# Hash attention and a sigmoid-GELU feed-forward on one Trainium2 core: the first pair of steps with one Strassen level, weight conversion handed out operation by operation, and another order of PSUM banks

## The chip, the cores and the metric

The kernel runs on one core of a Trainium2 chip. The metric is the device time of one execution in microseconds. A core has TensorE (PE, matmuls into PSUM), VectorE (DVE), ScalarE (ACT) and GpSimd (POOL), each with its own queue that it works off in order, and DMA queues that are fed by issuing engines; here nearly all transfers are issued by SyncE (SP), one after the other. Engines wait for each other through semaphores. [...]

## The reference

```python
# q, k, v: (4, 8, 768, 64); proj: (64, 6); w_in: (512, 2048); w_out: (2048, 512), the weights in double precision
q_bucket, k_bucket = ...                      # 6 sign bits of q @ proj and k @ proj, as a number
scores = where(q_bucket == k_bucket, q @ k.T / sqrt(64), -1e9)
attn = softmax(scores) @ v
x = attn.transpose(0, 2, 1, 3).reshape(3072, 512)
h = x @ w_in
return (h * 1 / (1 + exp(-1.702 * h))) @ w_out
```

All arithmetic is float32. The first half of the program is the attention, the second the two products of the feed-forward; the change is in the first of these two.

## The kernel before

**Attention** (to about 316 us). Sixteen pairs of heads; at the end `xT` holds x transposed, 512 x 3072. VectorE normalizes the result of the last pair of heads (`invert`, `norm`, L492 to L506) after PE has started on the feed-forward. The weights come as doubles and are converted to floats by `convert` in chunks of 128 x 512: one load of 512 KB (`raw`, L162), then six VectorE operations (L178 or L180, L182, L186 or L188, L193, L195, L198) and one square on ScalarE (L190). There is one `raw` buffer, so a chunk can be loaded only when L193 and the square of the chunk before it are done. Fourteen chunks of w_in are converted during attention; the last two (`LATE`) and the sixteen of w_out during the feed-forward.

**First product, h = x @ w_in** (`feed_forward`, 316 to 625 us). It is made in three blocks of 1024 tokens, and in each block in eight steps of 128 rows in each half of h, 24 steps in all, numbered n. One level of Strassen-Winograd turns a step into seven products (`product`, L739, each two matmul instructions of 128x128x512), whose operands are sums of quarters of w_in (`in_sums`, on GpSimd) and of x (`sums_b`, on VectorE). Results are gathered in SBUF tiles u, v, c21 and c22 by copies on ScalarE and adds on VectorE (`add`, L749); ScalarE applies the activation (`emit`, L746); GpSimd makes the four outer sums that the second product will want of them (`g_outer`, L219 to L222); and each result goes to HBM (`keep`, L743) on SyncE's queue.

There are two forms of a step. `hidden` (L930) makes all seven products whole. `pair_of_steps` (L828) makes two steps at once, and in it products 2 and 3 of both steps together are done by a second level of Strassen (`nested`, L789): seven small products of 128x128x256 (L800) each in place of four whole products for the two. They want sums of their own, of weights (`nest_w`, on GpSimd) and of x (`nest_x`, on VectorE). They accumulate in only two PSUM banks (pool `inner`, tags a and x), so most small products wait until VectorE has added the one before on the same bank. The first small product of product 3 is made at the end of its pair; the other six are put on the list `behind` and made between the products of the next pair. The completion of v (`done3`) then releases ScalarE's activation and GpSimd's eight outer sums for both steps.

Steps 0 to 19 are ten such pairs, and steps 20 to 23 use `hidden`. Its products take PSUM banks in turn (`bank`, L719): four of the pool `outer` and four of `sets`.

**What orders the work.** The instructions of PE, VectorE, ScalarE and GpSimd run in the order in which the program issues them. Extra work is put between the products at numbered hooks (`on`, L1148): hook 1 stands after a pair's first product, hook 2 after the second, 3 and 4 after the two products 6, 5 after the first small product of product 2, 6 and 7 after the products 7, 8 after the products 5 and their adds, 9 and 10 after the products 4, hook 10 at the very end. The table `todo` says which step gets a conversion, a sum for the second product, and so on. `conversions` (L1093) walks the chunks; it starts the load of the next chunk with the first operations of the present one, and stops twice in a chunk, so that one call issues operations one to three and the next call four to six. SyncE's queue is not written by hand: a planner puts each transfer into it.

Of the kernel before, what the change touches and what calls it, by code (L numbers as in the profile page):

```python
# [8 lines left out]
F32 = mybir.dt.float32  # L9
# [10 lines left out]
P = 128  # L20
# [18 lines left out]
def kernel(  # L39
# [166 lines left out]
    LATE = 2  # L206
# [29 lines left out]
    def in_sums(t):  # L236
        return sums_a(nc.gpsimd, *quarters_in(slice(2 * t * P, (2 * t + 2) * P)))
# [457 lines left out]
    def feed_forward(tag, late=()):  # L695
# [9 lines left out]
        with ExitStack() as fctx:  # L705
# [5 lines left out]
            inner_ctx = fctx.enter_context(ExitStack())  # L711
            inner = inner_ctx.enter_context(tc.tile_pool(name=f"in{tag}", bufs=1, space=PSUM, side="right"))
# [217 lines left out]
            def hidden(sb, mt, mid=(), end=()):  # L930
                n = sb * MT + mt
                first = n not in heads
                a, u = heads.pop(n) if n in heads else head(n)
# [30 lines left out]
                if not first and n + 1 < n1 * MT:  # L964
# [140 lines left out]
            for t in range(NESTED):  # L1105
                sb, at = divmod(t, MT // 2)
                hooks = {}
                steps_of = pair_of_steps(t, hooks)
                if t == 0:
                    next(steps_of)  # L1110
                    yield
                    twice = twice_ctx.enter_context(tc.tile_pool(name=f"tw{tag}", bufs=1, side="right"))
                    wop = fctx.enter_context(tc.tile_pool(name=f"wo{tag}", bufs=1))
                    cv_ctx = fctx.enter_context(ExitStack())
                    cv = cv_ctx.enter_context(tc.tile_pool(name=f"cv{tag}", bufs=1))
                    cps = cv_ctx.enter_context(tc.tile_pool(name=f"cps{tag}", bufs=1, space=PSUM))


                    w_out_sb = wop.tile([P, 4, FC, P], F32, name="w_out_sb")
                    wqs += [w_out_sb[:, 2 * i : 2 * i + 2, MT * k : MT * (k + 1), :] for i in range(2) for k in range(2)]  # L1120
                    wqs += [xT[:, i, 0 : 4 * XT].rearrange("p (h c d) -> p h c d", h=2, d=P) for i in range(3)]

                    order = [8 * k + 4 * c + i for c in range(2) for k in range(2) for i in range(4)]
                    chunks = [(w_out_sb[:, :, fc, :].rearrange("p r x -> p x r"), wo[fc]) for fc in order]
                    steps = conversions(cv, cps, late + chunks)
                    free = [i for i in range(LATE + 1, 3 * MT) if i % MT != MT - 1]
                    for i in (list(range(1, LATE + 1)) if late else []) + free[:FC]:
                        todo[i] = [lambda: next(steps)] * 2
                    low, high = (sums_a(nc.vector, *(x[:, :, F4 * c : F4 * (c + 1), :] for x in wqs)) for c in range(2))
                    first = 2 * MT + 1  # L1130
                    for i, f in enumerate(low):
                        todo[first + i] = todo[first + i] + [f]
                    todo[first + 1] = todo[first + 1] + inner_sums(0)[:2]
                    todo[first + 2] = todo[first + 2] + inner_sums(0)[2:]
                    todo[first + 4] = high + inner_sums(1)
                    todo[first + 5] = inner_sums(2)
                    todo[first + 6] = inner_sums(3)


                    places = [[w_out_sb[:, r, 4:8, :].rearrange("p c d -> p (c d)") for r in range(4)],  # L1140
                              [xT[:, k, XT * j : XT * (j + 1)] for k in (1, 0) for j in range(2)],
                              [xT[:, k, XT * j : XT * (j + 1)] for k, j in ((2, 1), (0, 3), (1, 3), (1, 1))]]
                    places = [[x[:, j * TH : (j + 1) * TH] for x in y for j in range(2)] for y in places]
                    more = nest_x(0, places[0])
                    hooks[3] = more[2] + nest_w(0)
                    hooks[4] = more[3]

                def on(i, fs):  # L1148
                    hooks[i] = hooks.get(i, []) + fs

                if at == 0 and sb > 0:
                    on(1, more[2])
                    on(3, more[3][:2])
                    on(4, more[3][2:])
# [4 lines left out]
                x = todo.pop(2 * t + 1, [])  # L1159
                on(7, x[0:1])  # L1160
                on(9, x[1:2])
                on(10, x[2:])
                if t + 1 < MT // 2:
                    on(5, in_sums(t + 1))
                    on(8, nest_w(t + 1))
                if at == MT // 2 - 1:
                    x = sums_b(nc.vector, *quarters_x(sb + 1))
                    more = nest_x(sb + 1, places[sb + 1])
                    on(8, x[0:1])
                    on(9, x[1:2])  # L1170
                    on(10, x[2:4])
                whole(steps_of)
                yield
            nesting[0] = False
            for n in range(2 * NESTED, 3 * MT):
                sb, mt = divmod(n, MT)
                if n == 2 * NESTED + 1:
# [119 lines left out]
```

## Time and profile before

| | |
|---|---|
| median of three runs | 892.74 us (891.35 to 893.68) |
| profiled execution | 891.65 us, span 889.5 us |
| feed-forward, first product | 316.5 to 624.9 us |
| second product | 624.9 us to the end |

The page of the profile gives for each engine its busy time, for each pair of engines who waited for whom, and groups of instructions by the line that issued them. A row such as `L739 PE MATMUL product<-xT,w_in_sb` names line, engine, operation, output and inputs. In lists in order of time the first two numbers are start and duration in microseconds; in brackets stands the idle time before it on that engine and what ended it. One matmul instruction on floats shows as two records, so a product of two instructions shows as x4 and a small product as x2, and the recorded duration overlaps with the next one's start by 0.16 us.

### The profile page before, as it was taken

How to read it: one execution, taken by the hardware profiler on the slowest of the kernel's cores; microseconds unless marked ns; L12 is line 12 of the kernel's file. 1: busy time of each engine (PE TensorE's matmuls, PEld its weight loads, DVE VectorE, ACT ScalarE, POOL GpSimd, SP SyncE). 2: the span in 40 equal slices, each digit the busy share in tenths (PEclk: the TensorE clock that was granted, in tenths of full speed). 3: DMA queues.
4: the chain of work that ended last, by engine and by line, in shares of the span. 5: the costliest groups of instructions: out<-in, count | busy, mean ns of one | idle time of the engine just before them, and what ended most of it. 6: DMA issues, size and time to landing. Idle time of an engine off the chain costs nothing.

```text
span 889.5 us, 13736 instructions
## 1 busy us (share of the span) xinstructions
PE 858.9 (97%) x4965; PEld 522.4 (59%) x4965; DVE 705.7 (79%) x1068; ACT 340.5 (38%) x567; POOL 324.5 (36%) x291
## 2 busy tenths in 40 slices
PE   9999999999999979999999999989999999999996
PEld 4444444444444435555555554534888888888885
DVE  4589999999999886667866697547797978797786
ACT  5866677766677523433333333333100000000000
POOL 4242243332343463876443333778923100000000
PEclk9999999999999998999999999989999999999998
DMA  5536545665542103554455546566655485477534
GB/s 129 95 58 112 89 82 83 111 109 99 84 83 80 34 25 99 208 194 156 167 193 196 195 157 210 189 208 241 219 230 189 159 225 206 168 223 233 197 105 98
DMA packets 169164, 132.12 MB, mean 149 GB/s; under 512 B 123616, under 2 KB 138112, under 8 KB 163712
## 3 DMA queue, kind: packets, MB, share of 16 engines
q1 hardware_dynamic: 166528, 129.70, 51.2%
q10 hardware_dynamic: 2560, 1.46, 0.7%
q8 instruction: 41, 0.67, 0.3%
q14 instruction: 35, 0.29, 0.1%
HBM read 79.69 MB, written 50.33 MB: 146 GB/s over the span
## 4 chain that ended last, share of the span: by engine, by line
PE 74%; DVE 13%; POOL 4%; issue 4%; DMA 3%; ACT 1%; SPq 0%; ACTq 0%; DVEq 0%; POOLq 0%
PE product L1056 26%; PE ps L432 17%; PE av L465 13%; PE product L739 12%; PE small L800 3%; DMA raw<-in_moe_w_out_dram 3%; DVE xT L1060 1%; DVE v L749 1%; PE dn L486 1%; PE hash L408 1%; DVE w_out_sb L195 1%; POOL t L222 1%; POOL t L221 1%; POOL t L219 1%; DVE bits L182 1%
## 5 line engine op out<-in xcount | busy, mean ns | idle before, releaser
L433 ACT ACTIVATE e<-ps 128x768 f32<-128x768 f32 x192 | 151.3, 812 | 25.6 <-PE ps L432 23.1
L432 PE MATMUL ps<-qT,kT 64*128 64x384 f32 x768 | 155.1, 482 | 0.0
L465 PE MATMUL av<-e,v 128*32 128x385 f32 x1536 | 128.0, 487 | 0.0
L440 POOL TENSOR_TENSOR acc<-e 128x768 f32<-128x768 f32 x32 | 51.8, 1618 | 194.3 <-ACT e L433 174.8
L739 PE MATMUL product<-xT,w_in_sb 128*128 128x512 f32 x208 | 99.7, 607 | 0.0
L739 PE MATMUL product<-t_x,s_in 128*128 128x512 f32 x192 | 91.5, 603 | 4.2 <-DVE w_out_sb L198 4.1
L465 PEld LDWEIGHTS av<-e,v 128*32 128x32 f32 x1536 | 48.5, 109 | 76.3 <-issue 74.6
L432 PEld LDWEIGHTS ps<-qT,kT 64*128 64x128 f32 x768 | 68.0, 187 | 38.5 <-issue 38.4
L219 POOL TENSOR_TENSOR t<-v,u 128x512 f32<-128x512 f32 x24 | 33.3, 1386 | 125.3 <-ACT v L746 125.3
L1069 ACT COPY u<-product 128x256 f32<-128x256 f32 x21 | 7.8, 372 | 174.0 <-PE product L1056 140.8
L432 PE MATMUL ps<-qf,kf 64*128 64x384 bf16 x384 | 62.9, 324 | 0.1
L739 PEld LDWEIGHTS product<-xT,w_in_sb 128*128 128x128 f32 x208 | 40.6, 196 | 33.8 <-issue 31.5
L739 PEld LDWEIGHTS product<-t_x,s_in 128*128 128x128 f32 x192 | 36.9, 193 | 34.8 <-issue 26.6
L441 POOL TENSOR_TENSOR acc<-acc,e 128x768 f32<-128x768 f32 x32 | 55.8, 1744 | 2.5
L446 DVE SCALAR_TENSOR_TENSOR acc<-e 128x768 f32<-128x768 f32 x32 | 47.7, 1490 | 5.1 <-ACT e L433 5.1
L749 DVE TENSOR_TENSOR v<-small,v 128x256 f32<-128x256 f32 x70 | 28.9, 418 | 24.3 <-PE small L800 24.3
L739 PE MATMUL product<-t_x,w_in_sb 128*128 128x512 f32 x96 | 45.2, 593 | 0.0
L749 DVE TENSOR_TENSOR u<-small,u 128x256 f32<-128x256 f32 x70 | 28.5, 417 | 16.3 <-PE small L800 8.0
L432 PEld LDWEIGHTS <-kf 64*128 64x128 bf16 x384 | 18.9, 94 | 35.1 <-issue 6.2
L448 DVE TENSOR_TENSOR acc<-acc,e 128x768 f32<-128x768 f32 x32 | 34.3, 1072 | 3.3
L448 DVE TENSOR_TENSOR acc<-acc,acc 128x768 f32<-128x768 f32 x32 | 31.7, 991 | 6.3 <-POOL acc L441 3.2
L1056 PE MATMUL product<-raw_g,xT 128*128 128x256 f32 x152 | 35.1, 379 | 0.0
(241 smaller groups left out, 1648.6 us busy)
## 6 DMA issues: line engine op xcount, KB each, us to landing
raw_g<-g_dram SPq DMA_DIRECT2D x22, 1024.0 KB
s_in<-g_dram SPq DMA_DIRECT2D x20, 1024.0 KB
g_dram<-t SPq DMA_DIRECT2D x72, 256.0 KB
g_dram<-c SPq DMA_DIRECT2D x48, 256.0 KB
raw<-in_moe_w_in_dram SPq DMA_DIRECT2D x16, 512.0 KB
raw<-in_moe_w_out_dram SPq DMA_DIRECT2D x16, 512.0 KB
v<-in_v_dram SPq DMA_DIRECT2D x32, 192.0 KB
g_dram<-u SPq DMA_DIRECT2D x24, 256.0 KB
```

The costliest lines, as they stand in the source:

```text
L219: return [lambda: eng.tensor_tensor(t1, b12, b11, op=Alu.subtract), lambda: eng.tensor_tensor(b12, b22, b12, op=Alu.subtract), lambda: eng ...
L432: nc.tensor.matmul(ps[:, j, 0:HS], a[hs, keys], m[hs, cols], start=not last, stop=last)
L433: nc.scalar.activation(es[c][:, kt, :, 0:HS], ps[:, :, 0:HS], Act.Exp, scale=1.0 / D**0.5)
L440: nc.gpsimd.tensor_tensor(acc, es[c][:, 0, :, 0:HS], es[c][:, 1, :, 0:HS], op=Alu.add)
L441: nc.gpsimd.tensor_tensor(acc, acc, es[c][:, 2, :, 0:HS], op=Alu.add)
L446: nc.vector.scalar_tensor_tensor(acc, e[0], T * TINY, e[1], op0=Alu.add, op1=Alu.add)
L448: nc.vector.tensor_tensor(acc, acc, x, op=Alu.add)
L465: nc.tensor.matmul(av[D * j + d : D * j + d + 32, :], vt[:, t, j, d : d + 32], es[c][:, t, j, :], start=(t == 0), stop=(t == T - 1))
L739: nc.tensor.matmul(ps, wq[LEFT[i]][:, kc, :], xq[RIGHT[i]][:, kc, :], start=(start and kc == 0), stop=(kc == K2 - 1), skip_group_check=not ...
L749: nc.vector.tensor_tensor(dst, x, y, op=Alu.add)
L800: nc.tensor.matmul(ps[at], wq[LEFT[i]], xq[RIGHT[i]], start=start, stop=True, skip_group_check=not start)
L1056: nc.tensor.matmul(ps, wq[LEFT[i]][:, c, :], gq[RIGHT[i]][:, c, :], start=(c == 0), stop=(c == F4 - 1))
```

## The change

Three things change in `feed_forward`.

1. Steps 0 and 1 are made by `hidden`. They borrow a pool of two banks (`f1`), which is closed after step 1; then the pool `inner` is opened in its place. Only pairs 1 to 9 (`NESTED = range(1, MT + 2)`) use the second level. The sums of x for it, and those of the weights for pair 1, are issued within step 1; those of the weights for pair 0 move to pair 3, since the first pair of the next block uses them. In the new order of SyncE's queue the loads of the two late chunks of w_in stand behind the stores of step 0 and of step 1, and in most pairs the first load of a chunk stands behind one more store, that of u.
2. `conversions` stops after each operation. A chunk takes six calls, at hooks 1, 2, 2, 3, 3, 4 in a pair's first half and 6, 7, 7, 9, 9, 10 in its second, where it was two calls at 2 and 3, or 7 and 9. The last sum of x for a new block moves from hook 10 to hook 1 of the next pair, and the eight inner sums of x are spread over hooks 1 to 9, one at each but hook 3.
3. For steps 21 to 23 the two new bank pools change places: the first (`f2`) lies where `inner` was, the second (`f3`) where the conversion's tiles were. Before, the first lay on the conversion's.

```diff
-            NESTED = 2 * MT // 2 + 2
-            sets, todo, turn = [], {}, [-1]
+            NESTED = range(1, MT + 2)
+            sets = [small_ctx.enter_context(tc.tile_pool(name=f"f1{tag}", bufs=1, space=PSUM, side="right"))]
+            todo, turn = {}, [-1]
...
-                    for at, _ in enumerate(x):
-                        if at == 2:
-                            yield
+                    for _ in x:
+                        yield
                     yield
...
-            for t in range(NESTED):
+            hidden(0, 0, in_sums(1))
+            yield
...
-                        todo[i] = [lambda: next(steps)] * 2
+                todo[i] = [lambda: next(steps)] * 6
...
-                    hooks[3] = more[2] + nest_w(0)
-                    hooks[4] = more[3]
+            more = nest_x(0, places[0])
+            hidden(0, 1, nest_w(1) + more[2], more[3] + todo.pop(1, []))
+            yield
+            small_ctx.close()
+            inner_ctx = fctx.enter_context(ExitStack())
+            inner = inner_ctx.enter_context(tc.tile_pool(name=f"in{tag}", bufs=1, space=PSUM, side="right"))
+            nesting[0] = True
+            for t in NESTED:
...
-                x = todo.pop(2 * t, [])
-                on(2, x[0:1])
-                on(3, x[1:2])
-                on(5, x[2:])
...
+                for n, places_of in ((2 * t, (1, 2, 2, 3, 3, 4)), (2 * t + 1, (6, 7, 7, 9, 9, 10))):
+                    x = todo.pop(n, [])
+                    for i in places_of:
+                        on(i, *x[:1])
+                        x = x[1:]
+                    on(5 if n % 2 == 0 else 10, *x)
...
+                elif t + 1 == MT // 2:
+                    on(5, *nest_w(0))
...
-                    sets += [fctx.enter_context(tc.tile_pool(name=f"f{i}{tag}", bufs=1, space=PSUM)) for i in (1, 2)]
+                    sets[:] = [fctx.enter_context(tc.tile_pool(name=f"f{2 + i}{tag}", bufs=1, space=PSUM, side=side))
+                               for i, side in enumerate(("right", "left"))]
```

More of the change, by code (lines that the diff above doesn't have):

```diff
@@ L710, in feed_forward @@
             outer = fctx.enter_context(tc.tile_pool(name=f"f0{tag}", bufs=2, space=PSUM, side="right"))
-            inner_ctx = fctx.enter_context(ExitStack())
-            inner = inner_ctx.enter_context(tc.tile_pool(name=f"in{tag}", bufs=1, space=PSUM, side="right"))
+            small_ctx = fctx.enter_context(ExitStack())
+            inner = None
             twice_ctx = fctx.enter_context(ExitStack())
@@ L963, in hidden @@
                 keep(sb, mt, 0, u)
-                if not first and n + 1 < n1 * MT:
+                if not first and n + 1 < n1 * MT and (n + 1) // 2 not in NESTED:
                     heads[n + 1] = head(n + 1)
@@ L1099, in conversions, with on @@
                         next(y)
-                    for at, _ in enumerate(x):
-                        if at == 2:
-                            yield
+                    for _ in x:
+                        yield
                     yield
-            for t in range(NESTED):
+            def on(i, *fs):
+                hooks[i] = hooks.get(i, []) + list(fs)
+            hidden(0, 0, in_sums(1))
+            yield
+            twice = twice_ctx.enter_context(tc.tile_pool(name=f"tw{tag}", bufs=1, side="right"))
@@ new lines, in feed_forward @@
+            wop = fctx.enter_context(tc.tile_pool(name=f"wo{tag}", bufs=1))
+            cv_ctx = fctx.enter_context(ExitStack())
+            cv = cv_ctx.enter_context(tc.tile_pool(name=f"cv{tag}", bufs=1))
+            cps = cv_ctx.enter_context(tc.tile_pool(name=f"cps{tag}", bufs=1, space=PSUM))
+            w_out_sb = wop.tile([P, 4, FC, P], F32, name="w_out_sb")
+            wqs += [w_out_sb[:, 2 * i : 2 * i + 2, MT * k : MT * (k + 1), :] for i in range(2) for k in range(2)]
+            wqs += [xT[:, i, 0 : 4 * XT].rearrange("p (h c d) -> p h c d", h=2, d=P) for i in range(3)]
@@ new lines, in feed_forward @@
+            order = [8 * k + 4 * c + i for c in range(2) for k in range(2) for i in range(4)]
+            chunks = [(w_out_sb[:, :, fc, :].rearrange("p r x -> p x r"), wo[fc]) for fc in order]
+            steps = conversions(cv, cps, late + chunks)
+            free = [i for i in range(LATE + 1, 3 * MT) if i % MT != MT - 1]
+            for i in (list(range(1, LATE + 1)) if late else []) + free[:FC]:
+                todo[i] = [lambda: next(steps)] * 6
+            low, high = (sums_a(nc.vector, *(x[:, :, F4 * c : F4 * (c + 1), :] for x in wqs)) for c in range(2))
@@ new lines, in feed_forward @@
+            first = 2 * MT + 1
+            for i, f in enumerate(low):
+                todo[first + i] = todo[first + i] + [f]
+            todo[first + 1] = todo[first + 1] + inner_sums(0)[:2]
+            todo[first + 2] = todo[first + 2] + inner_sums(0)[2:]
+            todo[first + 4] = high + inner_sums(1)
+            todo[first + 5] = inner_sums(2)
+            todo[first + 6] = inner_sums(3)
+            places = [[w_out_sb[:, r, 4:8, :].rearrange("p c d -> p (c d)") for r in range(4)],
+                      [xT[:, k, XT * j : XT * (j + 1)] for k in (1, 0) for j in range(2)],
+                      [xT[:, k, XT * j : XT * (j + 1)] for k, j in ((2, 1), (0, 3), (1, 3), (1, 1))]]
@@ L1106, in feed_forward @@
+            places = [[x[:, j * TH : (j + 1) * TH] for x in y for j in range(2)] for y in places]
+            more = nest_x(0, places[0])
[6 more added lines that the diff above has]
+            for t in NESTED:
                 sb, at = divmod(t, MT // 2)
@@ L1107, in feed_forward @@
                 hooks = {}
[L1108 to L1127, printed above, removed]
-                        todo[i] = [lambda: next(steps)] * 2
[L1129 to L1144, printed above, removed]
-                    hooks[3] = more[2] + nest_w(0)
-                    hooks[4] = more[3]
@@ L1148, in on @@
[L1148 to L1154, printed above, removed]
-                x = todo.pop(2 * t, [])
-                on(2, x[0:1])
-                on(3, x[1:2])
-                on(5, x[2:])
[L1159 to L1162, printed above, removed]
+                if at == 0:
+                    on(1, x_sums[3], more[2][0])
+                    for i, f in zip((2, 4, 5, 6, 7, 8, 9), more[2][1:] + more[3]):
+                        on(i, f)
@@ L1166, in feed_forward @@
                 if at == MT // 2 - 1:
-                    x = sums_b(nc.vector, *quarters_x(sb + 1))
+                    x_sums = sums_b(nc.vector, *quarters_x(sb + 1))
                     more = nest_x(sb + 1, places[sb + 1])
[L1169 to L1172, printed above, removed]
+                    for i in range(3):
+                        on(8 + i, x_sums[i])
+                whole(pair_of_steps(t, hooks))
@@ L1173, in feed_forward @@
                 yield
-            nesting[0] = False
-            for n in range(2 * NESTED, 3 * MT):
+            turn[0] = -1
+            for n in range(2 * NESTED.stop, 3 * MT):
                 sb, mt = divmod(n, MT)
-                if n == 2 * NESTED + 1:
+                if n == 2 * NESTED.stop + 1:
                     assert not behind
```

5 lines of the change are left out of this document (3 added, 2 removed).

## The prediction

> **What bounds the kernel now.** I read the page's busy times, then who waited for whom on PE, then the order in time of every engine in the first half of the feed-forward (316 to 625 us), the only stretch that the change touches.
>
> ```profile
> PE 858.9 (97%) x4965; PEld 522.4 (59%) x4965; DVE 705.7 (79%) x1068; ACT 340.5 (38%) x567; POOL 324.5 (36%) x291
> PE small L800 <- DVE v L749: 9.1, 9, 2.0
> PE small L800 <- issue: 5.2, 1, 5.2
> PE product L739 <- DVE w_out_sb L198: 4.1, 1, 4.1
> ```
>
> PE is busy 97% of the span, so time is won only where it waits: 9.1 us in nine waits for VectorE's adds, 5.2 in the first pair of steps, 4.1 in the bank wait of step 21. The two long ones cost more than their idle time (busy time by stretch; the last three columns are granted clock, DMA share and GB/s):
>
> ```profile
> 330.50:333.00 2.50, 0.00 (x0) 0.01 (x1) 2.50 (x6) 0.00 (x0) 2.34 (x5) 0.82 0.01 3
> 335.00:337.00 2.00, 2.00 (x4) 0.87 (x3) 0.42 (x1) 0.00 (x0) 1.92 (x2) 0.50 0.35 131
> 337.00:339.00 2.00, 2.00 (x4) 0.98 (x3) 0.00 (x0) 0.49 (x2) 1.84 (x5) 0.52 0.00 0
> 588.00:590.00 2.00, 0.75 (x1) 0.50 (x2) 1.90 (x3) 0.00 (x0) 1.92 (x3) 0.53 0.68 253
> 594.00:596.00 2.00, 2.00 (x4) 0.74 (x4) 0.00 (x0) 0.21 (x1) 1.70 (x2) 0.77 0.73 270
> ```
>
> The clock is at half from about 332.1 to 338.9 and from 588.1 to 594.9 (0.82 over 2.5 us is 0.9 us at half, 0.77 over 2.0 is 0.9, and so on): 6.8 us each time. PE is at work from 333.0 and 589.25 in them, so half of 5.9 and of 5.7 us, 2.9 and 2.8, is lost besides the idle time.
>
> **Part A: the first two steps (to the start of pair 2).** PE in order of time:
>
> ```profile
> 316.45 3.70 PE L739 MATMUL product<-xT,w_in_sb 128*128 128x512 f32 x8
> 333.02 1.19 PE L800 MATMUL small<-w_out_sb,w 128*128 128x256 f32 x2 [5.16 <-issue]
> 341.18 1.88 PE L739 MATMUL product<-t_x,w_in_sb 128*128 128x512 f32 x4
> 342.90 0.59 PE L800 MATMUL small<-w_out_sb,w_in_sb 128*128 128x256 f32 x2
> 343.33 1.88 PE L739 MATMUL product<-t_x,w_in_sb 128*128 128x512 f32 x4
> 369.12 1.88 PE L739 MATMUL product<-xT,w_in_sb 128*128 128x512 f32 x4
> ```
>
> A product takes 1.72 us (341.18 to 342.90), a small one 0.43. A nested pair is 10 products and 14 small ones, 23.22; two unnested steps are 14 products, 24.08. The change adds 0.86 in all. It removes the stall: unnested steps need neither the inner sums of x (eight VectorE adds that stand behind the last normalization, L506) nor those of the weights. Starting at 316.45 as before, with 0.5 allowed for ScalarE's first copy, step 1 would end at 341.0; pair 1 has no third product left over from pair 0 (six small ones, 2.58), so it takes 20.64 and pair 2 would start at 361.6, not 369.12: **-7.5**. The adds of step 0 now stand ahead of the last normalization on VectorE; nothing waits for that but the inner sums, due in pair 1.
>
> But the order of the DMA queue changes. SyncE issues in order, and the loads of the last two chunks of w_in move behind the stores of steps 0 and 1:
>
> ```profile
> 327.42 0.34 SPq L162 DMA_DIRECT2D raw<-in_moe_w_in_dram  x1
> 344.58 0.33 SPq L162 DMA_DIRECT2D raw<-in_moe_w_in_dram  x1
> 351.18 0.68 DVE L180 TENSOR_SCALAR part<-raw 128x512 uint32<-128x512 uint32 x1
> 355.67 0.41 DVE L749 TENSOR_TENSOR v<-small,v 128x256 f32<-128x256 f32 x1
> 457.44 1.27 POOL L219 TENSOR_TENSOR t<-v,u 128x512 f32<-128x512 f32 x1 [13.98 <-ACT v L746]
> 466.53 1.28 POOL L222 TENSOR_TENSOR t<-c,t 128x512 f32<-128x512 f32 x1
> 468.24 1.37 SPq L743 DMA_DIRECT2D g_dram<-c  x3
> 469.70 0.50 SPq L162 DMA_DIRECT2D raw<-in_moe_w_out_dram  x1
> 470.30 0.57 SPq L743 DMA_DIRECT2D g_dram<-u  x1
> 474.32 0.69 DVE L180 TENSOR_SCALAR part<-raw 128x512 uint32<-128x512 uint32 x1 [1.00 <-DMA raw<-in_moe_w_out_dram]
> ```
>
> Before, both loads were issued by 344.6 and nothing waited. Now the second comes behind the four outer sums of step 1 on GpSimd: v is complete at 341.0 + 0.7 (an add) + 0.8 (emission) = 342.5, the sums take half of 457.44 to 467.81, 5.2, so the load is issued at 348.0 to 349. A load that is waited for lands 4.6 us after its issue (469.70 to 474.32): 353.2. All six operations of that chunk stand ahead of pair 1's first adds on VectorE, 4.2 us (351.18 to 355.67 less one add), then two adds, 1.0: 358.4. The second small product of pair 1 needs them and would be due at 351.8. **+6.6.** On ScalarE the chunk's square waits for the same load, with pair 1's copies queued behind it, so PE stands idle about 4 us from 350.2, does one product and stands again. An idle of 4.1 closed the clock at 588, so I take half clock for 6.8 us again; most falls into the wait, and of the rest, some 2.4 us of work, half counts: **+1.2**. [...]
>
> A: -7.5 + 6.6 + 1.2 = **+0.3**; bounds -7.5 (the load in time) and +2.
>
> The weights' inner sums of pair 0 (eight of 128x128) move on GpSimd's queue to pair 3, behind its outer sums; a quarter of an outer sum's elements each, they end some 5 us into pair 4, whose second small product is the first to need them, 13.3 in: nothing. If GpSimd were later than that, pair 4 would wait for the rest.
>
> **Part B: pairs 2 to 9, conversions handed out singly.**
>
> ```profile
> 450.17 0.70 DVE L180 TENSOR_SCALAR part<-raw 128x512 uint32<-128x512 uint32 x1 [1.89 <-DMA raw<-in_moe_w_out_dram]
> 454.42 1.03 DVE L198 SCALAR_TENSOR_TENSOR w_out_sb<-size,w_out_sb 128x512 f32<-128x512 f32 x1
> 455.35 0.42 DVE L749 TENSOR_TENSOR v<-small,v 128x256 f32<-128x256 f32 x1
> 455.68 0.68 DVE L749 TENSOR_TENSOR v<-product,v 128x512 f32<-128x512 f32 x1
> 456.28 0.41 DVE L749 TENSOR_TENSOR v<-small,v 128x256 f32<-128x256 f32 x1
> 498.48 0.70 DVE L180 TENSOR_SCALAR part<-raw 128x512 uint32<-128x512 uint32 x1 [0.99 <-DMA raw<-in_moe_w_out_dram]
> 543.84 0.49 SPq L162 DMA_DIRECT2D raw<-in_moe_w_out_dram  x1
> 548.98 0.69 DVE L180 TENSOR_SCALAR part<-raw 128x512 uint32<-128x512 uint32 x1 [2.33 <-DMA raw<-in_moe_w_out_dram]
> 393.67 1.88 PE L739 MATMUL product<-xT,w_in_sb 128*128 128x512 f32 x4
> 417.94 1.88 PE L739 MATMUL product<-xT,w_in_sb 128*128 128x512 f32 x4
> 442.93 1.88 PE L739 MATMUL product<-xT,w_in_sb 128*128 128x512 f32 x4
> 566.76 1.45 PE L739 MATMUL product<-xT,w_in_sb 128*128 128x512 f32 x3
> ```
>
> Eight pairs take 197.6 us (369.12 to 566.76), 11.9 over their 185.8 of work. It looks as if three conversion operations in a row delay the add at 455.35 that PE waits for, and moving L198 (0.93) behind it would give that back each time. But the pairs run in a ring: load lands 450.17, conversion and adds to 456.69 (6.5), emission 0.75, eight outer sums to 467.81 (10.4), last store, three stores, next load issued 469.70 (1.9), landing 474.32 (4.6): 24.15 in all, and 24.16 to the landing after it, at 498.48. L198 stays in the ring, since the add at 456.28 that completes v is still behind it. The ring grows by one add that now stands behind the first conversion operation (0.33, from 455.35 to 455.68) and by a store of u that now goes ahead of the load (0.55): 25.0. Pairs 5, 6, 7 and 9 take 25.0; pair 3, whose load lands some 7.0 in and whose add then comes 5.0 later against 11.2 due, 24.1. Pair 4 has its chunk loaded half a pair early, since pair 3 ends without one, and its VectorE sums for the next tokens spread over the hooks: I take 23.5 where it took 25.0 (417.94 to 442.93), and the same for pair 8, built alike. Pair 2 finds no outer sums ahead of its load: 23.2 where it took 24.6 (369.12 to 393.67). Sum 194.3, **-3.3**. If the store's 256 KB also delay the load itself (an estimate: 512 KB land in 4.6 behind 768 KB of stores, so a fifth more data is some 0.7), five pairs grow by 0.7: 0. Between these I take **-1.7**; bounds -5 (ring unchanged) and +4.
>
> **Part C: other banks last.**
>
> ```profile
> 583.30 1.88 PE L739 MATMUL product<-t_x,s_in 128*128 128x512 f32 x4
> 589.25 3.78 PE L739 MATMUL product<-t_x,s_in 128*128 128x512 f32 x4 [4.07 <-DVE w_out_sb L198]
> 588.16 1.04 DVE L198 SCALAR_TENSOR_TENSOR w_out_sb<-size,w_out_sb 128x512 f32<-128x512 f32 x1
> ```
>
> Step 21's product 5 takes the bank that the conversion leaves at 589.2. Now it takes one of the inner products' banks, free since pair 9's last inner product was added, and the conversion's banks are first used by the head of step 22, four products later: 583.30 + 4 x 1.72 = 590.2, 1.0 after L198. Gone: 4.07 and the half clock's 2.8, **-6.9**; the other end is -2, if that head waits instead. The sums on GpSimd behind step 21's v move up with it.
>
> **Sum:** +0.3 - 1.7 - 6.9 = -8.3. The profiled execution's 891.65 (span 889.5) becomes 883.4; the runs' median lies 1.1 above it, so 884.4 on 892.74.
>
> **Rivals.**
> 1. The first pair gains in full: the second late load lands before pair 1 needs it. For it: PE's 7.5 us are there. Against: the queue's order. A falls by 7.8: 876.6.
> 2. The bank wait moves to the head of step 22 instead of going, no clock dip: only 1.0 spare. C -2: 889.3.
> 3. Slower: the load ring. If a store ahead of the load costs more than its issue, every ring pair pays. Pairs 2, 4 and 8 give -4.4, A and C -6.6; so the five others, 24.6 on average now, must each take 27.3 for +2.7: a landing of 7 in place of 4.6 decides, and at 7.5 the time would be 898. For it: the store does go ahead. Against: waited loads landed in 4.6 (469.70) to 5.1 (543.84).
> 4. The change doesn't spread anything, since the ring sets the pace (B +0, the rest as forecast): 886.1, inside the range.
>
> **How the numbers follow.** 0.3% (2.7 us) is about what a measurement tells from no change. Forecast with 4: 0.58, own range 881 to 888.5; rival 1: 0.12; rival 2: 0.13, half of it within 0.3%; rival 3: 0.12; the rest, 0.05, even. Faster 0.58 + 0.12 + 0.06 = 0.77 with rounding, same 0.09, slower 0.14. The range, 876.5 to 891, leaves out rival 3 and the tails.
>
> **What would show it.** A: no wait for inner sums near 330; a wait of 6 to 7 us at pair 1's first small products, ended by VectorE behind a load of w_in, and pair 2 starting within 2 us of 369. B: pairs 5 to 7 at 25 us, their first conversion operation waiting for its load, pairs 4 and 8 near 23.5. C: no wait on L198 before step 21's product 5, clock at full from there to the end of this half. Wrong if pair 1 runs through (lower), if ring pairs pass 26 (higher), or if the head of step 22 waits.

## The result and the profile after

The changed kernel takes 883.02 us, the median of four runs (882.75 to 883.30), against 893.20 for the kernel before (four runs, 891.35 to 893.68): a ratio of 0.989 with a 95% interval of 0.9873 to 0.9907. The profiled execution took 883.3, its span is 881.4. Forecast were 884.4 for the median and 883.4 for the profiled execution.

The traces are divided here at three places that both show: the first product of the feed-forward, the start of pair 2, and the start of step 20. The "step 20" column ends where the second product's first matmul starts.

| in us | start | first two steps | pairs 2 to 9 | step 20 to 23 | second product |
|---|---|---|---|---|---|
| before | 316.45 | 52.67 | 197.64 | 58.02 | 264.7 |
| after | 315.74 | 51.81 | 198.07 | 50.98 | 264.8 |
| difference | -0.71 | -0.86 | +0.43 | -7.04 | +0.1 |
| forecast | 0 | +0.3 | -1.7 | -6.9 | 0 |

Of the 8.1 us by which the spans differ, 7.0 come from step 20 to 23, whose banks were changed, and 0.7 from the start, which the change does not touch (in the traces of the experiments it lies between 315.3 and 316.8). The first two steps and pairs 2 to 9 leave 0.4 between them, which is less than two traces of the same code can differ by, as the experiments show.

The busy time of PE on the page of the changed kernel, and then who waited for whom on PE (total, count, longest):

```profile
PE 855.8 (97%) x4953; PEld 517.1 (59%) x4953; DVE 709.9 (81%) x1056; ACT 340.6 (39%) x567; POOL 330.8 (38%) x291
```

```profile
PE small L801 <- DVE v L750: 8.9, 9, 2.5
PE product L740 <- ACT v L843: 3.6, 1, 3.6
```

The wait of 5.16 for the inner sums and that of 4.07 for L198 are gone. In their place stands one of 3.6. The nine waits for VectorE's adds, which the second part was to shorten, come to the same total, 8.9 for 9.1, but the longest is now 2.5 where it was 2.0. PE of the changed kernel in order of time, at the places where the chain turns:

```profile
315.74 1.98 PE L740 MATMUL product<-xT,w_in_sb 128*128 128x512 f32 x4
340.50 3.60 PE L740 MATMUL product<-xT,w_in_sb 128*128 128x512 f32 x8
353.42 3.68 PE L740 MATMUL product<-xT,w_in_sb 128*128 128x512 f32 x4 [3.61 <-ACT v L843]
357.58 0.67 PE L801 MATMUL small<-w_out_sb,w 128*128 128x256 f32 x2 [0.49 <-issue]
367.55 1.88 PE L740 MATMUL product<-xT,w_in_sb 128*128 128x512 f32 x4
474.86 0.70 PE L801 MATMUL small<-xT,s_in 128*128 128x256 f32 x2 [2.49 <-DVE v L750]
501.12 0.70 PE L801 MATMUL small<-xT,s_in 128*128 128x256 f32 x2 [1.74 <-DVE v L750]
565.62 1.88 PE L740 MATMUL product<-xT,w_in_sb 128*128 128x512 f32 x4
582.15 3.60 PE L740 MATMUL product<-t_x,s_in 128*128 128x512 f32 x8
585.60 5.42 PE L740 MATMUL product<-xT,w_in_sb 128*128 128x512 f32 x12
616.60 1.67 PE L1058 MATMUL product<-raw_g,w_out_sb 128*128 128x256 f32 x7
```

SyncE's queue (start, and the time that the issues took):

```profile
348.13 0.37 SPq L162 DMA_DIRECT2D raw<-in_moe_w_in_dram  x1
441.88 0.59 SPq L162 DMA_DIRECT2D raw<-in_moe_w_out_dram  x1
464.79 2.34 SPq L744 DMA_DIRECT2D g_dram<-c  x3
467.22 0.41 SPq L744 DMA_DIRECT2D g_dram<-u  x1
467.73 0.40 SPq L162 DMA_DIRECT2D raw<-in_moe_w_out_dram  x1
494.04 0.45 SPq L162 DMA_DIRECT2D raw<-in_moe_w_out_dram  x1
```

VectorE, which starts on a chunk when its load has landed, and the add in pair 1 that PE waits for:

```profile
352.16 0.69 DVE L180 TENSOR_SCALAR part<-raw 128x512 uint32<-128x512 uint32 x1 [2.66 <-DMA raw<-in_moe_w_in_dram]
357.06 0.41 DVE L750 TENSOR_TENSOR u<-small,u 128x256 f32<-128x256 f32 x1
446.77 0.69 DVE L180 TENSOR_SCALAR part<-raw 128x512 uint32<-128x512 uint32 x1 [4.53 <-DMA raw<-in_moe_w_out_dram]
473.78 0.70 DVE L180 TENSOR_SCALAR part<-raw 128x512 uint32<-128x512 uint32 x1 [6.97 <-DMA raw<-in_moe_w_out_dram]
500.05 0.69 DVE L180 TENSOR_SCALAR part<-raw 128x512 uint32<-128x512 uint32 x1 [6.21 <-DMA raw<-in_moe_w_out_dram]
587.03 1.06 DVE L198 SCALAR_TENSOR_TENSOR w_out_sb<-size,w_out_sb 128x512 f32<-128x512 f32 x1
```

Two things are to be seen. First, the late load: issued at 348.13, landed at 352.16, its conversion and two adds end at 357.5, and only then does the second small product start. Second, the ring: the loads that pairs 5, 6 and 7 wait for land 4.9, 6.05 and 6.0 us after their issue, and VectorE stands still for 4.5 to 7.0 us in front of each. GpSimd closes the ring:

```profile
453.97 1.27 POOL L219 TENSOR_TENSOR t<-v,u 128x512 f32<-128x512 f32 x1 [14.60 <-ACT v L747]
463.07 1.28 POOL L222 TENSOR_TENSOR t<-c,t 128x512 f32<-128x512 f32 x1
480.99 1.27 POOL L219 TENSOR_TENSOR t<-v,u 128x512 f32<-128x512 f32 x1 [16.64 <-ACT v L747]
```

From landing to the first outer sum 7.2 (446.77 to 453.97), the eight sums 10.4 (to 464.35), the stores of c and u 3.4 (to 467.73), the landing 6.05 (to 473.78): 27.0 in all, and pair 6 takes 27.0.

### The profile page after: what moved, and what is told of

The parts are those of the page before. It is cut to its first block, busy times and chain, and to the rows that moved or that the text cites. A ratio compares the mean times of both kernels' runs of the same rounds, so it can differ in the third digit from the quotient of the medians.

```text
span 881.4 us, 13702 instructions
## 1 busy us (share of the span) xinstructions
PE 855.8 (97%) x4953; PEld 517.1 (59%) x4953; DVE 709.9 (81%) x1056; ACT 340.6 (39%) x567; POOL 330.8 (38%) x291
## 4 chain that ended last, share of the span: by engine, by line
PE 36%; issue 6%; DVE 5%; POOL 5%; DMA 1%; SPq 0%; ACT 0%; ACTq 0%; POOLq 0%; DVEq 0%
PE product L1058 26%; PE product L740 9%; PE small L801 2%; DVE xT L1062 1%; POOL t L222 1%; POOL t L221 1%; DMA raw<-in_moe_w_out_dram 1%; POOL t L219 1%; POOL v L220 1%; DVE v L750 1%; DVE y L1038 1%; DVE w_out_sb L195 0%; DVE v L1062 0%; DVE t2a L221 0%; DVE raw_g L220 0%
## 5 line engine op out<-in xcount | busy, mean ns | idle before, releaser
L433 ACT ACTIVATE e<-ps 128x768 f32<-128x768 f32 x192 | 151.2, 812 | 25.7 <-PE ps L432 23.1
L740 PE MATMUL product<-xT,w_in_sb 128*128 128x512 f32 x216 | 102.0, 602 | 3.6 <-ACT v L843 3.6
L740 PE MATMUL product<-t_x,s_in 128*128 128x512 f32 x192 | 89.4, 593 | 0.2 <-ACT u L928 0.2
L221 POOL TENSOR_TENSOR t<-c,t 128x512 f32<-128x512 f32 x24 | 35.0, 1457 | 0.0
L222 POOL TENSOR_TENSOR t<-c,t 128x512 f32<-128x512 f32 x24 | 34.2, 1427 | 1.9
```

Source lines behind the costliest of these rows:

```text
L221: lambda: eng.tensor_tensor(t2, b22, t1, op=Alu.subtract),
L222: lambda: eng.tensor_tensor(t4, b21, t2, op=Alu.subtract)]
L433: nc.scalar.activation(es[c][:, kt, :, 0:HS], ps[:, :, 0:HS], Act.Exp, scale=1.0 / D**0.5)
L740: nc.tensor.matmul(ps, wq[LEFT[i]][:, kc, :], xq[RIGHT[i]][:, kc, :], start=(start and kc == 0), stop=(kc == K2 - 1), skip_group_check=not ...
```

## The experiments

Ten kernels were run, each one step away from the kernel before or from the changed one, or adding such steps up. All compute the whole of the reference. The last three columns are from one profiled execution of each, in us, divided as above.

| kernel | median us | before, same chip | ratio (95%) | first two steps | pairs 2 to 9 | steps 20 to 23 |
|---|---|---|---|---|---|---|
| banks only | 885.14 | 894.51 | 0.9903 (0.9865 to 0.9941) | 52.6 | 198.6 | 51.0 |
| old banks | 890.18 | 891.83 | 0.9983 (0.9965 to 1.0002) | 52.7 | 196.8 | 56.9 |
| two calls | 882.75 | 894.51 | 0.9872 (0.9838 to 0.9906) | 52.6 | 196.8 | 51.0 |
| singles only | 892.03 | 890.99 | 1.0006 (0.9990 to 1.0021) | 52.7 | 200.0 | 56.8 |
| u on ScalarE | 881.63 | 891.83 | 0.9867 (0.9831 to 0.9902) | 53.7 | 195.4 | 51.0 |
| loads on ScalarE | 875.00 | 894.51 | 0.9791 (0.9759 to 0.9823) | 52.6 | 187.9 | 51.0 |
| early late load | 882.37 | 894.51 | 0.9878 (0.9845 to 0.9911) | 49.0 | 198.1 | 51.0 |
| ... and moved | 876.36 | 891.83 | 0.9817 (0.9783 to 0.9850) | 45.95 | 196.9 | 51.0 |
| all | 867.48 | 891.83 | 0.9716 (0.9685 to 0.9747) | 45.9 | 187.2 | 51.0 |
| all, two calls | 871.19 | 890.99 | 0.9780 (0.9757 to 0.9804) | 45.9 | 190.1 | 51.0 |

The chips' own times for the kernel before differ by up to 3.5 us, so small differences between kernels of different chips are read from the last three columns. These have a spread of their own. In pairs 2 to 9 the kernel before and the one with the banks only run the same code, and their sums are 197.6 and 198.6; so do the changed kernel and the one with the old banks, with 198.1 and 196.8. A difference of 1.3 in that column therefore shows nothing.

**Banks only and old banks.** The kernel before with the third part alone:

```diff
-sets += [... tile_pool(name=f"f{i}{tag}", bufs=1, space=PSUM) for i in (1, 2)]
+sets += [... tile_pool(name=f"f{i}{tag}", bufs=1, space=PSUM, side=side)
+         for i, side in ((1, "right"), (2, "left"))]
```

> The kernel before with the third part alone: for steps 21 to 23 the first new pool lies where the inner products' banks were, the second where the conversion's were. Theory (the bank wait and the clock dip behind it are a cost of their own, 7.0 of the 8.1 us by which the two traces differ): no wait at step 21's product 5, step 20 to the second product falls from 58.0 to about 51, time 893.2 - 7.0 = 886.2, between 885.5 and 887. Rival (the gain of that stretch needs the other two parts, because they shift what VectorE does in steps 20 and 21): the wait comes back at the head of step 22, or the clock still dips, time 889 to 893.

and the changed kernel without it:

```diff
-for i, side in enumerate(("right", "left"))]
+for i, side in enumerate(("left", "right"))]
```

> The changed kernel with its third part alone undone: the first pool of steps 21 to 23 lies on the conversion's banks again, the second where the inner products' were. Theory (the banks carry nearly the whole gain, the other two parts together about 1): a wait of some 4 for L198 before step 21's product 5 and a clock at half behind it, time 883.0 + 7 = 890, between 888.5 and 891.5, so hardly faster than the kernel before. Rival (the other parts have moved the last conversion early enough that the old order would not wait any more): below 886.

Alone, the part gives the changed kernel's time (0.9903 against 0.989). Without it, what is left of the gain is 0.17%, and the interval holds 1. PE and VectorE of the kernel with the old banks:

```profile
582.21 1.88 PE L740 MATMUL product<-t_x,s_in 128*128 128x512 f32 x4
588.15 3.64 PE L740 MATMUL product<-t_x,s_in 128*128 128x512 f32 x4 [4.06 <-DVE w_out_sb L198]
```

```profile
587.06 1.03 DVE L198 SCALAR_TENSOR_TENSOR w_out_sb<-size,w_out_sb 128x512 f32<-128x512 f32 x1
```

The last operation of the conversion starts at 587.06 there and at 587.03 in the changed kernel. So the conversion is not earlier; the product no longer asks for its bank. Both times were near what the theory expected (885.14 for 886.2, a little below the range of 885.5 to 887; 890.18 for 890), and the stretch itself took 51.0 and 56.9 us, so the banks are settled as the source.

**Two calls.** The changed kernel, conversions again in threes:

```diff
-todo[i] = [lambda: next(steps)] * 6
+todo[i] = [lambda: [next(steps) for _ in range(3)]] * 2
-... ((2 * t, (1, 2, 2, 3, 3, 4)), (2 * t + 1, (6, 7, 7, 9, 9, 10))):
+... ((2 * t, (2, 3)), (2 * t + 1, (7, 9))):
```

> The changed kernel with its second part undone for the conversions alone: a chunk is again issued in two calls of three operations, at hooks 2 and 3 or 7 and 9; the spread sums of x, the first pair and the banks stay as changed. Theory (handing out singly lengthens the ring of load, conversion, v, outer sums, stores, since the store of u goes ahead of the load and an add stands behind the first operation): pairs 5, 6 and 7 fall back from 25.1, 27.0 and 26.3 to 24.2 to 25.0, pair 9 stays at 25.4, time 883.0 - 5 = 878, between 876.5 and 880. Rival (as forecast, the single operations let adds through and save some 1.7, or at least cost nothing): 883 to 886.

The theory expected 878 and failed: 882.75, the changed kernel's time. Its pairs 5 to 7 take 25.3, 27.1 and 23.2. Pair 6 holds a spell at half clock. PE of this kernel, and the clock over the stretches of one microsecond behind the wait (PE, weight load, VectorE, ScalarE, GpSimd busy; the granted clock is the third number from the end):

```profile
479.28 1.12 PE L801 MATMUL small<-xT,w_in_sb 128*128 128x256 f32 x2 [1.89 <-DVE v L750]
480.19 3.19 PE L740 MATMUL product<-xT,w_in_sb 128*128 128x512 f32 x4
```

```profile
479.00:480.00 1.00, 0.72 (x2) 0.63 (x3) 1.00 (x3) 0.63 (x1) 0.00 (x0) 0.71 0.65 262
480.00:481.00 1.00, 1.00 (x2) 0.43 (x2) 0.58 (x2) 0.63 (x1) 0.11 (x1) 0.50 0.00 0
482.00:483.00 1.00, 1.00 (x3) 0.47 (x2) 0.00 (x0) 0.00 (x0) 0.92 (x2) 0.58 0.01 2
```

The clock was at half from about 479.4 to 482.8 behind a wait of 1.9, which costs about 1.7 (an estimate: half of the 3.4 at half clock). Without that the pairs would sum to some 195 (an estimate: 196.8 less 1.7). But the spell hardly explains the time: the other three executions, with mean granted clocks of 0.993 and 0.994 against 0.991 in the profiled one, took 881.07 to 883.37. The run shows no difference between the two ways of handing out, so the question was put the other way round.

**Singles only.** The kernel before with the second part alone (the sums of x are left as they were); the diff, put in short, shows the calls of a pair's first half, and besides, `conversions` stops after each operation as in the change:

```diff
-todo[i] = [lambda: next(steps)] * 2
+todo[i] = [lambda: next(steps)] * 6
-on(2, x[0:1]); on(3, x[1:2]); on(5, x[2:])
+for i in (1, 2, 2, 3, 3, 4): on(i, x[0:1]); x = x[1:]
```

> The kernel before with the second part alone, for the conversions: six single calls at hooks 1, 2, 2, 3, 3, 4 and 6, 7, 7, 9, 9, 10 in place of two calls of three; the sums of x, the first pair and the banks as before. In SyncE's order u's store then stands ahead of the first load in most pairs, as in the changed kernel. Theory (the ring sets the pace, so letting adds through wins nothing, and the store ahead of the load costs): pairs 2 to 9 sum to 198 to 202 in place of 197.6, pairs 5 to 7 above 25, time the same as before or up to 4 longer, 893 to 897 on a baseline of 893. Rival (forecast's first reading: the adds of the inner products no longer wait behind three operations): pairs shorter, time 2 to 5 below the kernel before.

The pairs sum to 200.0, 2.4 more than in the kernel before and 1.4 more than in the kernel with the banks only, and the time is 1.0006 (0.9990 to 1.0021) of the kernel before: at most 0.1% won or 0.2% lost. SyncE and VectorE of this kernel at pair 6:

```profile
471.19 0.60 SPq L162 DMA_DIRECT2D raw<-in_moe_w_out_dram  x1
```

```profile
476.68 0.70 DVE L180 TENSOR_SCALAR part<-raw 128x512 uint32<-128x512 uint32 x1 [5.62 <-DMA raw<-in_moe_w_out_dram]
```

The load takes 5.5 behind the store of u, where it took 4.6 in the kernel before; that of pair 7, behind such a store too, takes 5.0. The rival, a time 2 to 5 lower because adds no longer wait, is refuted for this order of the queue.

**The store of u on ScalarE's queue.** The changed kernel:

```diff
-keep(sb, mts[i], 0, u[i])
+nc.scalar.dma_start(out=g_dram[len(LEFT) * sb, :, mts[i], :], in_=u[i])
```

> The changed kernel with the stores of u from the pairs issued on ScalarE's queue, right behind u's activation, so that none stands ahead of a load on SyncE's queue; operations are still handed out singly. Theory (pairs 5 to 7 are longer than forecast because the store of u goes ahead of the load: 0.5 of issue and some 1.4 of landing): the loads that the pairs wait for land in 4.6 to 4.9, pairs 5, 6 and 7 take 24.2 to 25.0 in place of 25.1, 27.0 and 26.3, time 883.0 - 3.5 = 879.5, between 878 and 881. Rival (u's bytes move at the same time whichever queue issues them, and the landing is as long): landings of 6.0 remain, pairs 6 and 7 above 26, time 882 or more.

Pairs 5 to 7 take 24.7, 25.7 and 24.7, and their loads land in 5.1, 4.6 and 5.15. The pairs sum to 195.4, 2.7 less. So far that is the theory's direction. But pair 3 takes 25.8 in place of 24.6, and its load, with no store of u ahead of it on SyncE's queue, lands 6.3 after its issue, later than any load that a pair of the changed kernel waits for:

```profile
395.22 0.92 SPq L162 DMA_DIRECT2D raw<-in_moe_w_out_dram  x1
401.53 0.69 DVE L180 TENSOR_SCALAR part<-raw 128x512 uint32<-128x512 uint32 x1 [5.34 <-DMA raw<-in_moe_w_out_dram]
```

Nor does the landing follow u's place in the other traces. With two calls the load of pair 6 stands ahead of the store of u and still lands in 5.8:

```profile
467.80 0.51 SPq L162 DMA_DIRECT2D raw<-in_moe_w_out_dram  x1
473.62 0.70 DVE L180 TENSOR_SCALAR part<-raw 128x512 uint32<-128x512 uint32 x1 [2.22 <-DMA raw<-in_moe_w_out_dram]
```

With the old banks, where the order is that of the changed kernel, the loads of pairs 5 to 7 land in 4.7, 4.75 and 5.9. The time, 881.63 (879.99 to 883.20), lies a little above the expected 878 to 881; the first two steps took 1.9 longer in the profiled execution, with the clock at half from 354.9 to 361.8. So it is not shown that the store of u ahead of the load makes the landings long: the landing varies from 4.7 to 6.05 with it and from 4.6 to 6.3 without it, and what is left of the 2.7 beyond the traces' own spread of 1.3 is little.

**The loads on ScalarE's queue.** The changed kernel, with the load of the next chunk issued behind the fourth operation of the present one:

```diff
-gens = [convert(cv, *x, psum=psum) for x in chunks]
+gens = [convert(cv, *x, queue=nc.scalar if i >= len(late) else None, psum=psum) for i, x in enumerate(chunks)]
...
-    for y in gens[i + 1 : i + 2]:
-        next(y)
-    for _ in x:
+    for k, _ in enumerate(x):
+        if k == 3:
+            for y in gens[i + 1 : i + 2]:
+                next(y)
```

> The changed kernel with the loads of w_out's chunks issued on ScalarE's queue, right behind the fourth operation and the square of the chunk before, in place of SyncE's queue behind the stores; still one buffer, the late chunks of w_in load as in the changed kernel. Theory (pairs 3 to 9 run in a ring that closes over SyncE's stores, which wait for GpSimd): the ring is cut, the first conversion operation no longer waits for its load for more than 1 us, pairs 3, 5, 6, 7 and 9 fall to 23.2 to 23.8, their sum with the others from 198.1 to about 188, time 883.0 - 10 = 873, between 871 and 876. Rival (the pairs are long because VectorE's queue holds the adds behind the conversion operations, wherever the load is): pairs stay above 24.3, time 880 or more.

The pairs sum to 187.9 for an expected 188, and the time is 875.0 for an expected 873. ScalarE and VectorE of this kernel at pair 6:

```profile
461.43 0.36 ACTq L162 DMA_DIRECT2D raw<-in_moe_w_out_dram  x1
```

```profile
465.83 0.68 DVE L180 TENSOR_SCALAR part<-raw 128x512 uint32<-128x512 uint32 x1
```

The load leaves while GpSimd is still at its outer sums (to 462.7) and before SyncE issues the stores of c and u (from 463.2), and VectorE starts on the chunk without a wait. Besides the queue, only the place in the program at which the load is issued was changed, so the loads' place behind the stores in SyncE's queue is shown to be what made the pairs long. On SyncE's queue the load stood behind stores that waited for GpSimd (at pair 6 of the changed kernel the last outer sum ends at 464.35, the stores are issued from 464.79 on and the load at 467.73); with the load on the other queue the eight pairs take 10.2 us less, 187.9 for 198.1.

**The late load early.** The changed kernel, where the second late chunk of w_in has a room of its own, in a part of w_out's tile that is written only later; SyncE then issues it right behind the first:

```diff
-raw = cv.tile([P, CW, 2], U32, tag="raw", name="raw")
+raw = cv.tile([P, CW, 2], U32, tag="raw", name="raw") if room is None else room
...
+late[1:] = [(*x, w_out_sb[:, 3, MT:FC, :].rearrange("p c (d two) -> p (c d) two", two=2).bitcast(U32)) for x in late[1:]]
```

> The changed kernel, but the second of the two late chunks of w_in is loaded into a part of w_out's tile that is written only from step 8 on, so that its load need not wait for the first chunk's conversion; in SyncE's queue it then stands right behind the first late load, ahead of the stores of step 1. Theory (the first pair's gain is eaten by this load alone): step 1 still ends at 340.5, pair 1 runs through in about 20.7, pair 2 starts at about 361.2 in place of 367.6, no clock dip at 353, time 883.0 - 6.4 = 876.6, between 875.5 and 878.5. Rival (another wait takes its place: the inner sums of x and of the weights, or VectorE's six operations that stand before pair 1's adds): pair 2 starts after 364, time 880 or more.

The rival came true. Pair 2 starts 2.8 earlier, not 6.4, and the time falls by less than the runs can tell. VectorE and PE of this kernel:

```profile
345.34 0.68 DVE L180 TENSOR_SCALAR part<-raw 128x512 uint32<-128x512 uint32 x1
353.32 0.69 DVE L198 SCALAR_TENSOR_TENSOR w_in_sb<-size,w_in_sb 128x512 f32<-128x512 f32 x1
353.93 0.68 DVE L750 TENSOR_TENSOR v<-product,v 128x512 f32<-128x512 f32 x1
```

```profile
350.95 1.98 PE L740 MATMUL product<-xT,w_in_sb 128*128 128x512 f32 x4 [0.41 <-ACT v L843]
355.04 0.67 PE L801 MATMUL small<-w_out_sb,w 128*128 128x256 f32 x2 [2.10 <-issue]
```

The load is there, but the twelve operations of the two late chunks fill VectorE from 345.3 to 354.0 without a gap, with pair 1's first adds behind them. The second run adds the remedy: the second chunk's operations go behind those adds, and the sums of w_in that need them behind the operations.

```diff
-... ((2 * t, (1, 2, 2, 3, 3, 4)), (2 * t + 1, (6, 7, 7, 9, 9, 10))):
+... ((2 * t, (5, 5, 6, 6, 7, 7) if t == 1 and late else ...), (2 * t + 1, (8, 8, 9, 9, 10, 10) if t == 1 and late else ...)):
-    on(5, *in_sums(t + 1))
+    on(8 if t == 1 and late else 5, *in_sums(t + 1))
```

> The changed kernel with the second late load early as in the run with a room of its own, and besides its six operations moved in pair 1 from hooks 1 to 4 to hooks 5, 6 and 7, behind the first add that the inner products wait for; the sums of w_in that need them move on GpSimd from hook 5 to hook 8, and the next chunk's six operations to hooks 8 to 10. Theory (with the load in time, what was left of the first pair's wait, 2.1 and 0.8 of short ones, was twelve conversion operations in a row on VectorE): no wait above 0.7 in pair 1, pair 2 starts about 46 after the feed-forward's start in place of 51.8, and 49.0 with the early load alone; time 883.0 - 5.5 = 877.5, between 876.5 and 879. Rival (the wait moves on once more: the sums of w_in come late for pair 2, or its first adds stand behind the operations at hook 10): pair 2 or 3 longer by over 2, time 880 or more.

Pair 2 starts 45.95 after the feed-forward's first product, as expected, and the time is 876.36, just below the expected 876.5 to 879. So 6.7 of the 7.5 us reckoned for the first pair were there to be had; two things stood in front of it one behind the other, the load's place in SyncE's queue and the operations' place in VectorE's.

**All together, and all with two calls.**

> The run before it (early second late load, its operations moved behind pair 1's first adds) and the loads of w_out's chunks on ScalarE's queue together. Theory (the first pair and the ring are separate costs): pair 2 starts about 46.3 after the feed-forward's start, pairs 2 to 9 sum to 188, time 875.0 - 6 = 869, between 868 and 871. Rival (the two overlap, since with the ring cut pair 2 no longer runs up against anything that the first pair's delay hid): 872 or more.

> The run with the early late load, its operations moved and the loads on ScalarE's queue, with w_out's conversions handed out again in three operations at a time, at hooks 2 and 3 or 7 and 9, from pair 2 on. Theory (only where the loads are in time does it matter how the operations are handed out; then three in a row, 2.1 to 2.8, keep back an add that PE waits for by some 0.5 to 1 in most pairs): pairs 2 to 9 sum to 191 to 195 in place of 187.2, time 867.5 + 4 to 7, 871.5 to 874.5. Rival (with loads in time there is room for three in a row as well): within 1.5 of 867.5.

The first adds the two gains up: 867.48, 2.8% below the kernel before (2.5 to 3.2), where the changed kernel is 1.1% below it. That is a little below the expected 868 to 871, and the rival is refuted. Who waited for whom on PE in it:

```profile
PE small L801 <- DVE v L750: 0.6, 1, 0.6
PE product L740 <- ACT u L838: 0.3, 1, 0.3
```

Of 8.9 us of waits for v's adds 0.6 are left. In threes again (at hooks 2 and 3, or 7 and 9, in the same kernel) the pairs sum to 190.1, the time is 871.19, and these waits are back in part:

```profile
PE small L801 <- DVE v L750: 3.0, 3, 1.3
```

So handing out the operations singly is worth 2.9 us by the traces, 3.7 by the medians (of two chips), once the loads are in time; before that no run shows a gain. The theory's sign was right, its size of 4 to 7 was too large, and the rival, no difference above 1.5, is outside both figures.

## Why the prediction was right, and where it was not

**The time** was met to 1.4 us, and the range with the highest chance is the one that came. That it was met so closely is in part luck: the terms A and B were off in opposite directions (-1.2 and +2.1), and 0.7 us came from a start that had nothing to do with the change. What carries the forecast is part C.

**Part C** was right in every step: no wait, no dip, the head of step 22 not held (the products run on from 582.15 through 585.60 without a gap, with a granted clock of 1.00 from 566 to 617), -7.04 for -6.9. The banks alone carry it. Rival 2 is refuted.

**Part A**: the late load's chain was right to about a microsecond at each point: issue 348.13 (348 to 349), landing 352.16 (353.2), adds 357.5 (358.4), PE idle from about 349.6. What failed in the profiled execution is the step "I take half clock for 6.8 us again", costing 1.2. The clock of the changed kernel over three stretches:

```profile
352.00:354.00 2.00, 0.58 (x1) 0.50 (x2) 1.77 (x3) 1.63 (x3) 0.00 (x0) 0.86 0.00 0
354.00:356.00 2.00, 2.00 (x3) 0.66 (x2) 1.83 (x4) 0.00 (x0) 0.00 (x0) 0.50 0.00 0
356.00:358.00 2.00, 1.51 (x4) 0.42 (x3) 1.73 (x4) 0.58 (x1) 1.29 (x2) 0.78 0.86 260
```

It was at half for 3.4 us (0.14 of 2.0 lost at half rate is 0.56, then 2.0, then 0.88), and PE did one product in that time while it had to wait for VectorE anyhow, so the dip cost nothing and A came to -0.9. Four other kernels with the same first pair show the longer spell; here the run with the loads on ScalarE's queue:

```profile
352.00:354.00 2.00, 0.00 (x0) 0.00 (x0) 1.22 (x2) 1.15 (x2) 0.00 (x0) 0.78 0.04 14
356.00:358.00 2.00, 1.78 (x3) 0.21 (x1) 1.90 (x4) 0.77 (x2) 0.79 (x1) 0.50 0.47 164
358.00:360.00 2.00, 1.83 (x5) 1.53 (x6) 1.18 (x3) 1.03 (x2) 1.92 (x3) 0.51 0.24 98
```

There it lasts 6.8, from 353.1 to 360.0, and the first two steps take 52.6, 52.6, 52.7 and 53.7, that is -0.1 to +1.0 against the kernel before. The forecast +0.3 lies among these. So the term was right in kind, and its size varies from one profiled execution to another between 0 and 1.9. Rival 1 named the load alone as the obstacle ("the second late load lands before pair 1 needs it"); the run with that load early shows that this would not have brought the gain in full, since VectorE's twelve operations come next. That step of the prediction, one cause for the whole +6.6, was too simple.

**Part B** was mis-sized. The ring is right: cutting it gives back 10 us. But spreading the operations gained nothing by itself, and B was +0.4 instead of -1.7; in the three other traces with these pairs (old banks and the two with the early late load) it is between -0.8 and +0.5. That is rival 4, B +0, which lies in the forecast's range. Of the ring's terms the landing, taken as 4.6, was 4.9 to 6.05, and the stores of one pair took 3.4 where 2.45 were reckoned (1.9 and u's 0.55; the three of c took 2.34 where 1.37 were). Pairs 6 and 7 came to 27.0 and 26.3 for 25.0, pair 3 to 24.6 for 24.1, while pairs 2, 4, 5, 8 and 9 came within 0.4 of their forecast. The added 0.33 for one more add did not show: from the landing to the first outer sum it is 7.2, where it was 7.3 (450.17 to 457.44). The end with the store's 256 KB lengthening the landing, which gave 0, was the better one by its size, but its reason is not shown, as the run with u on ScalarE's queue says; and a fifth of 4.6 is 0.9, not 0.7. Rival 3 was the direction of this trace, stopped at a landing of 6, short of the 7 from which it decides. The wait at a second small product (2.49 and 1.74), ahead of the usual one, was not foreseen as a wait of PE: the add behind the first operation (474.39 to 474.81 on VectorE) releases the bank.

What stays open: why the landing behind the same stores is 4.9 in one pair and 6.05 in the next, and 4.75 in another execution, and why the profiled execution of the changed kernel got the short clock spell.

## What to carry to other kernels

When a small operation is put off to let something by, look first at what the engine waits for: here VectorE waited for a load, the load for a place behind stores in SyncE's queue, and those stores for GpSimd, so spreading VectorE's work showed no gain until the load left on another queue, and about 3 us then. A gain that a wait eats may have a second wait behind the first; work out the next one as if the first were gone. And a resource that a tile merely borrows (a PSUM bank that the conversion held) can be worth more than the work on it: swapping two pools gave 7 of 8 us.

## What the runs showed of the hardware

The clock went to half beside shorter idles than the two of the kernel before (5.16 and 4.07, each with 6.8 us at half clock), and not always. Beside a wait of 1.89 (two calls, PE back at 479.28) the granted clock was at half for 3.4 us, from about 479.4 to 482.8, while it stayed at 1.00 beside waits of 2.49 (changed kernel, over 472 to 478) and 2.10 (early late load, over 352 to 358). Beside a wait of 3.61 it was at half for 3.4 us (changed kernel, from about 353.4 to 356.9), and beside waits of 3.5 to 3.9 in the four other kernels with the same first pair for 6.8 (loads on ScalarE's queue, from 353.1 to 360.0). So the length of the wait alone did not decide it: 1.89 had a spell where 2.49 had none, and 3.58 (u on ScalarE) had twice the spell of 3.61. What decides it, these runs do not show. The prediction's step from an idle of 4.1 to 6.8 us at half clock was an estimate from the two stalls of one trace.
